# HGRN2 attention into a PReLU feed-forward layer: the usual steps without the one-column product that reads the moved keys

## The chip, the cores and the metric

One core of one Trainium2 chip runs the whole program. The metric is the device time of one execution in microseconds (us), the median of several runs. All matmuls are in float32, each of which the profile shows as two passes of a weight load and a matmul.

## The reference

The first part is a gated linear recurrence over 768 positions, for 4 batches and 8 heads of 48 values. The second part takes its output, 3072 rows of 384, through a feed-forward layer with 2048 hidden values and a learned slope for negative ones.

```python
def _attn_ref(q, k, v, f_logit) -> np.ndarray:
    B, H, S, D = q.shape                       # 4, 8, 768, 48
    f = 1.0 / (1.0 + np.exp(-f_logit))
    state = np.zeros((B, H, D, D), dtype=np.float32)
    y = np.zeros_like(q)
    for t in range(S):
        state = f[:, :, t, :, None] * state + np.einsum('bhd,bhe->bhde', k[:, :, t], v[:, :, t])
        y[:, :, t] = np.einsum('bhd,bhde->bhe', q[:, :, t], state)
    return y.astype(np.float32)

def _moe_ref(x, w_in, w_out, alpha) -> np.ndarray:
    h = x @ w_in
    g = np.maximum(h, 0.0) + alpha * np.minimum(h, 0.0)
    return (g @ w_out).astype(np.float32)
```

## The kernel before

The work is cut into 12 steps. A step is one chunk of 128 positions for a pair of batches; steps 2c and 2c + 1 belong to chunk c. Each step goes through three parts. *Preparation* loads the chunk, takes the sigmoid and forms running products of the gates (ScalarE and VectorE). *Attention* computes scores between queries and keys, the chunk's contribution to the state, and the output. *Network* takes the outputs of the step, laid out as `xT`, through both layers of the feed-forward part.

The recurrence needs the keys of a chunk with positions, not dimensions, along the partitions. From step 2 on this is done in two moves. VectorE transposes 32x32 blocks (word `kt`), and sixteen DMAs per step on SyncE's queue (word `km`, line 468) bring the blocks to their places in the tile `ksn`: four partition groups of the source (a) by four of the target (b). The sixteen DMAs are told of by eight semaphores, each used twice.

`ksn` is read on TensorE in two places. The *state products* (word `pd`, line 635, 64 matmul instructions per step) multiply keys and values into a PSUM tile `state`; each reads 48 of `ksn`'s columns on 64 of its partitions, and so blocks of four of the sixteen DMAs, and the first four products together read all sixteen. The *landed product* (word `kw`, line 641) is a product of one column of the identity with the four columns 0, 32, 64 and 96 of `ksn` on all partitions, one from each of the sixteen blocks. Its result, one row of four values, is never used: it goes into the PSUM bank that the next hidden-layer product (`n3` of the step before) then overwrites. `first` takes that bank from `ahead`, or a new one if there is none.

```python
        def keys_landed():
            to = ahead[n - 1, 3] = bank(f"phk_{i}")
            nc.tensor.matmul(to[0:1, 0:4], lhsT=ident[:, 0:1], rhs=x["ksn"][:, 0, 0:128:32], start=True, stop=True,
                             skip_group_check=True)
```

The order of the work is not left to a planner. It is written out by hand as a list of words, each with its step, and the program is emitted in that order, so that it is the order in which each engine's queue holds its instructions; an engine waits at an instruction until what that instruction needs is there. `FIRST` gives the words of the opening up to the end of step 3's attention and of step 2's network. `USUAL` gives the words of one step, and is used for n = 4 to 12 with words for a step that doesn't exist dropped; a word with `-` belongs to step n - 1, one with `+` to step n + 1. So in the usual order the network of step n - 1 runs between the attention of step n.

The words around the change, as TensorE sees them: `x0`, `x1` are scores of step n; `n0-` to `n7-` are the hidden-layer products of step n - 1 (line 763, 12 matmul instructions with 128x256 outputs each); `of` is a product within the chunk (line 597, 64 short matmuls, results copied by `oc0`, `oc1`); `pd` is the state products. Of the other engines, `g` is ScalarE's share and `G` VectorE's share of the activation that follows each `n`; `S0-` is four VectorE sums over gates; `m0` is VectorE's update of the running state, kept in `vs`, from the state products (lines 657 and 661). `A1`, `B` and so on are the output-layer products (line 859). `FIRST` has one `kw` of its own, for step 2. For step 3 it has `of:3 pd:3` and no `kw`. Values for steps 1 to 4 are loaded on GpSimd's queue, for the others on SyncE's.

Of the kernel before, what the change touches and what calls it, by code (L numbers as in the profile page):

```python
# [52 lines left out]
"""  # L53

USUAL = """
r0 R0 x0 X0 n0- g0- G0- n1- g1- G1- r1 R1 x1 X1 n2- g2- G2- kw n3- g3- G3- S0- of oc0 oc1 pd m0 n4- g4- G4- ld+ sg+ kr+ qc+ l1+ l2+ l3+ c0+ c1+ c2+
c3+ n5- g5- G5- n6- g6- G6- n7- g7- G7- S1- sc+ A1- B- ka- le+ k4+ e2+ p00A p01A p02A p03A p10A p11A p12A p13A y0 y1 C1- D- u2- ke+ kt+ e3+ e4+ sa+
e5+ m1 z0A z1A mv A2- C2- d0- oa- e6+ km+ e7+ sb+ fs+ E- u3- b- d1- s00+ s01+ s10+ s11+ e-
"""
# [929 lines left out]
```

## Time and profile before

| | |
|---|---|
| median of 3 runs | 617.76 us (615.91 to 619.95) |
| span of the profiled execution | 613.4 us |
| mean granted TensorE clock | 0.999 |
| hidden-layer products, line 763, tiles `ph` and `phk` | 948 and 108 matmul instructions |
| matmuls of line 641 | 18 (two passes each of nine products) |
| matmuls of line 635 on the tile `state` | 704 |
| like points of successive steps from step 5 on | some 47.3 us apart |

The span runs from the first to the last instruction of the program; the time of a run also holds what lies around it, here some 4.4 us by the median.

In the profile an engine's row names line, operation and tiles, out<-in. PE is TensorE's matmuls, PEld its weight loads, which run beside them, and PEldq its sequencer. DVE is VectorE, ACT ScalarE, POOL GpSimd, SP SyncE. The number of an instruction's durations is minimum/median/maximum in ns. Matmuls on small parts of the array run beside each other, so a group's busy time is less than count times duration. In brackets stands idle time before a group and what ended it; "issue" means that no wait the profile knows of ended it.

### The profile page before, as it was taken

To read this page: it belongs to the slowest core of one execution; us is meant where nothing else is said; L and a number is where in the kernel's file an instruction comes from. 1 tells how busy PE (TensorE), PEld (TensorE's weight loads), DVE (VectorE), ACT (ScalarE), POOL (GpSimd) and SP (SyncE) were. 2 spreads that over 40 slices of the span, in tenths; PEclk is the share of its full clock that TensorE was granted. 3 is DMA by queue.
4 is the path that set the end of the run, shared out by engine and by line. 5 is a ranking of instruction groups with operands and counts; after the bars stand their busy time and mean duration, and the time that the engine had idled before them with its cause. 6 is when DMAs were issued, how large, how long until landed. Compare 5 with 4: busy or idle time off the path is not lost.

```text
span 613.4 us, 18759 instructions
## 1 busy us (share of the span) xinstructions
PE 586.4 (96%) x8042; PEld 526.6 (86%) x8042; DVE 485.3 (79%) x993; ACT 242.5 (40%) x464; POOL 109.5 (18%) x154
## 2 busy tenths in 40 slices
PE   1689899999999999999999999999999999999997
PEld 1589766898999799899899899889899889889997
DVE  7988899985588789799899799789799889762251
ACT  5887732523412352361272271361362263223110
POOL 7437566298050000000000000000000000000000
PEclk9999999999999999999999999999999999999999
DMA  8996343141002502502502502502602601201000
GB/s 272 322 337 186 103 142 53 41 136 24 14 25 45 153 10 43 158 2 49 161 1 50 159 2 47 162 2 42 168 1 39 162 11 35 47 2 27 26 1 26
DMA packets 72002, 50.40 MB, mean 82 GB/s; under 512 B 47248, under 2 KB 62480, under 8 KB 71920
## 3 DMA queue, kind: packets, MB, share of 16 engines
q1 hardware_dynamic: 64464, 38.77, 23.6%
q0 software_dynamic: 2944, 8.59, 4.8%
q10 hardware_dynamic: 4512, 1.85, 1.2%
q8 instruction: 63, 1.03, 0.8%
q14 instruction: 19, 0.16, 0.1%
HBM read 36.21 MB, written 4.72 MB: 67 GB/s over the span
## 4 chain that ended last, share of the span: by engine, by line
PE 84%; DVE 6%; ACT 3%; issue 2%; POOL 2%; DMA 2%; POOLq 0%; ACTq 0%; DVEq 0%
PE ph L763 32%; PE pc L859 10%; PE pa L859 9%; PE pe L859 5%; PE pd L859 5%; PE pb L859 5%; PE py L694 4%; PE phk L763 4%; PE qu L514 3%; PE raw L493 3%; DMA q<-in_qT 2%; PE ph L781 2%; PE state L635 2%; PE off L597 1%; DVE w_out_sb L211 1%
## 5 line engine op out<-in xcount | busy, mean ns | idle before, releaser
L763 PE MATMUL ph<-xT,w_in_sb 128*128 128x256 f32 x948 | 213.0, 382 | 0.0
L763 PEld LDWEIGHTS ph<-xT,w_in_sb 128*128 128x128 f32 x948 | 177.7, 190 | 27.0 <-issue 1.7
L769 ACT ACTIVATE neg<-ph 128x512 f32<-128x512 f32 x79 | 46.3, 597 | 146.7 <-PE ph L763 110.7
L773 DVE SCALAR_TENSOR_TENSOR gate<-neg,om,ph 128x256 f32<-128x256 f32 x158 | 67.7, 476 | 40.5 <-ACT neg L769 39.5
L731 POOL DMA_DIRECT2D xT<-y x22 | 11.9, 546 | 392.0 <-ACT y L703 392.0
L859 PE MATMUL pa<-w_out_sb,gate 128*128 128x192 f32 x352 | 61.9, 328 | 0.1
L859 PE MATMUL pc<-t,S 128*128 128x192 f32 x352 | 61.7, 329 | 0.0
L859 PEld LDWEIGHTS pa<-w_out_sb,gate 128*128 128x128 f32 x352 | 57.9, 190 | 2.0 <-DVE gate L773 1.3
L859 PEld LDWEIGHTS pc<-t,S 128*128 128x128 f32 x352 | 57.3, 190 | 0.8 <-issue 0.2
L522 DVE COPY_PREDICATED ad<-mquad,qu 128x224 f32<-128x224 int32 (+6 forms) x140 | 42.0, 300 | 9.3 <-PE qu L514 3.2
L501 DVE COPY_PREDICATED ad<-mraw,raw 128x256 f32<-128x256 int32 (+1 forms) x96 | 42.4, 441 | 7.0 <-POOL A L680 2.8
L345 ACT COPY ut<-qd 128x256 f32<-128x256 f32 (+1 forms) x52 | 32.0, 634 | 23.2 <-DVE qd L211 12.1
L211 DVE TENSOR_TENSOR ut<-ut,fs 128x512 f32<-128x512 f32 (+6 forms) x64 | 38.5, 604 | 3.3 <-POOL ut L211 2.4
L429 ACT COPY A<-q 48x512 f32<-48x512 f32 x40 | 24.7, 616 | 35.2 <-DVE q L211 31.9
L882 ACT ACTIVATE o<-pa 128x192 f32<-128x192 f32 x11 | 3.6, 330 | 76.9 <-PE pa L859 76.9
L493 PE MATMUL raw<-qd,k 48*32 48x80 f32 x1536 | 22.4, 243 | 10.3 <-DVE qd L211 10.3
L493 PEld LDWEIGHTS raw<-qd,k 48*32 48x32 f32 x1536 | 18.1, 109 | 15.7 <-issue 15.5
L680 ACT COPY A<-ad 32x256 f32<-32x256 f32 x75 | 30.1, 401 | 1.1
L859 PE MATMUL pe<-w_out_sb,S 128*128 128x192 f32 x176 | 30.5, 327 | 0.0
L859 PE MATMUL pb<-t,gate 128*128 128x192 f32 x176 | 30.4, 326 | 0.0
L859 PE MATMUL pd<-w_out_sb,S 128*128 128x192 f32 x176 | 30.4, 326 | 0.0
L694 PEld LDWEIGHTS py<-A,vs 128*64 128x64 f32 x768 | 26.0, 145 | 4.0 <-issue 2.2
(138 smaller groups left out, 894.3 us busy)
## 6 DMA issues: line engine op xcount, KB each, us to landing
w_out_raw<-in_w_out SPq DMA_DIRECT2D x8, 767.8 KB, 5.5
w_in_raw<-in_w_in SPq DMA_DIRECT2D x8, 767.2 KB, 12.1
out<-o SPq DMA_DIRECT2D x24, 192.0 KB, 2.1
f<-in_fT SPq DMA_DIRECT2D x7, 512.0 KB, 4.3
q<-in_qT SPq DMA_DIRECT2D x7, 512.0 KB, 5.2
k<-in_kT SPq DMA_DIRECT2D x7, 512.0 KB, 6.9
vs<-in_v SPq DMA_DIRECT2D x14, 192.0 KB, 6.9
ksn<-kt SPq DMA_DIRECT2D x80, 32.0 KB, 2.0
```

Of the source, the lines that this page charges most:

```text
L211: (nc.gpsimd if beside[0] else nc.vector).tensor_tensor(*a)
L345: w[f"c{r}{mark}"] = lambda r=r: nc.scalar.copy(q4()[:, gs, :, r], qdv[r][:, gs, :, 0])
L429: copy(A[halves(cc)[1], u0:u1, par * HP:(par + 1) * HP, CH * cc:CH * (cc + 1)], x["q3"][rows(par)].rearrange("p (u h c) s t -> p u h c (s ...
L493: nc.tensor.matmul(to[DB * j:DB * (j + 1), par, hp * C:hp * C + QW], lhsT=x["k"][r_, g * DB:(g + 1) * DB], rhs=qd[r_, g], start=True, stop ...
L501: nc.vector.copy_predicated(adu[:, :, :, d:4], mraw[:, d, :, d:4].bitcast(I32).unsqueeze(1).broadcast_to((128, H, NB, n_)), rv[:, :, QO[d] ...
L522: nc.vector.copy_predicated(ad[:, u, :, :, 4 * m:DB], mquad[:, lo:lo + n_].bitcast(I32).unsqueeze(1).unsqueeze(1).broadcast_to((128, 2, HP ...
L680: copy(A[s_, u, :, s_], ad[s_, u].rearrange("p r h t -> p (r h) t"))
L694: nc.tensor.matmul(to[64 * par:64 * par + 64, u, o:o + CH], lhsT=vs[bp][:, cc, u, hd * D:hd * D + 64], rhs=A[:, u, par * HP + hp, CH * cc: ...
L763: nc.tensor.matmul(ph[f][:, j * T:(j + 1) * T], lhsT=w_in_sb[:, kt, m * 128:(m + 1) * 128], rhs=x["T"][:, kt], start=(kt == 0 and j == 0), ...
L769: nc.scalar.activation(neg[f], ph[f].rearrange("p (j t) -> p j t", j=2), AF.Relu, scale=-1.0)
L773: nc.vector.scalar_tensor_tensor(gate[:, m % NH, m // NH], neg[f][:, j], om[:, m:m + 1], ph[f].rearrange("p (j t) -> p j t", j=2)[:, j], A ...
L859: nc.tensor.matmul(p[name][:, 0:DH], lhsT=of(f), rhs=by(f), start=(f == 0 and not more), stop=(f == NH - 1), skip_group_check=True)
```

## The change

The word `kw` is taken out of `USUAL`, where it stood between `G2-` and `n3-`. Nothing else is touched: `kw:2` stays in `FIRST`, and so does the code of `keys_landed`.

```diff
 USUAL = """
-r0 R0 x0 X0 n0- g0- G0- n1- g1- G1- r1 R1 x1 X1 n2- g2- G2- kw n3- g3- G3- S0- of oc0 oc1 pd m0 n4- g4- G4- ld+ sg+ kr+ qc+ l1+ l2+ l3+ c0+ c1+ c2+
+r0 R0 x0 X0 n0- g0- G0- n1- g1- G1- r1 R1 x1 X1 n2- g2- G2- n3- g3- G3- S0- of oc0 oc1 pd m0 n4- g4- G4- ld+ sg+ kr+ qc+ l1+ l2+ l3+ c0+ c1+ c2+
 c3+ n5- g5- G5- n6- g6- G6- n7- g7- G7- S1- sc+ A1- B- ka- le+ k4+ e2+ p00A p01A p02A p03A p10A p11A p12A p13A y0 y1 C1- D- u2- ke+ kt+ e3+ e4+ sa+
 e5+ m1 z0A z1A mv A2- C2- d0- oa- e6+ km+ e7+ sb+ fs+ E- u3- b- d1- s00+ s01+ s10+ s11+ e-
 """
```

So the landed product is no longer run in steps 4 to 11, eight of its nine uses. In these steps `first` finds no bank in `ahead` for `n3` and takes one itself, and the first instructions on TensorE that read `ksn` are the state products.

## The prediction

> **What bounds the kernel now.** I read the page's busy times first, then the chain that ended last, then TensorE's timeline around one use of the product that goes away.
>
> ```profile
> PE 586.4 (96%) x8042; PEld 526.6 (86%) x8042; DVE 485.3 (79%) x993; ACT 242.5 (40%) x464; POOL 109.5 (18%) x154
> ...
> PE 84%; DVE 6%; ACT 3%; issue 2%; POOL 2%; DMA 2%; POOLq 0%; ACTq 0%; DVEq 0%
> ```
>
> TensorE is busy for 96% of the 613.4 us span and makes 84% of the chain; in the usual steps it hardly waits for anyone. So whatever lengthens or shortens its own queue there goes into the span one for one. The next two answers are its timeline in step 5 (start, us, group) and the instructions of the removed line 641 in the same stretch. PEldq is TensorE's sequencer; an EVENT_SEMAPHORE is an instruction of its own that only waits.
>
> ```profile
> 241.71 5.45 PE L763 MATMUL ph<-xT,w_in_sb 128*128 128x256 f32 x24
> 247.08 0.92 PE L493 MATMUL raw<-qd,k 48*32 48x80 f32 x64
> ...
> 248.77 2.86 PE L763 MATMUL ph<-xT,w_in_sb 128*128 128x256 f32 x12
> 251.56 0.20 PE L641 MATMUL phk<-ksn,ident 128*1 128x4 f32 x2
> 251.68 2.86 PE L763 MATMUL phk<-xT,w_in_sb 128*128 128x256 f32 x12
> 254.47 0.32 PE L597 MATMUL off<-q,kh 48*32 48x32 f32 x14
> ```
>
> ```profile
> L641 PEldq EVENT_SEMAPHORE  x4: 51/51/51, 248.6 to 248.9; - x4
> L641 PEld LDWEIGHTS phk<-ksn,ident x2: 80/82/83, 251.6 to 251.6; 128*1 128x1 f32 x2
> ```
>
> The reader is to see two things. First, the product's four wait instructions run at 248.6 to 248.9, three microseconds ahead of the product itself (251.56): the sequencer has already queued the twelve long matmuls of n2, so these waits cost TensorE nothing. Second, what the product does cost: n0 and n1, two such groups side by side without it, take 247.08 - 241.71 = 5.37 us from start to next start; n2, kw and n3 take 254.47 - 248.77 = 5.70 us.
>
> Are those waits ever long? The queue of the keys' transfers says no.
>
> ```profile
> L468 SPq DMA_DIRECT2D ksn<-kt x16: 604/610/1965, 233.2 to 244.4; - x16
> ...
> DMA to landing us min/median/max: 1.9/2.0/3.9
> ```
>
> Step 5's last transfer is issued at 244.4 and the slowest needs 3.9 us, so all have landed by 248.3 at the latest; the product comes 3.2 us later, the state products that truly read the keys (line 635) at 255.2. Every one of the 32 wait instructions of line 641 takes 51 ns, the least. So no wait for data is removed or added; what moves is the instructions that do the waiting.
>
> **Removed.** Eight of nine uses (steps 4 to 11; step 2 keeps its own in the written-out order): per step four waits, two weight loads, two matmuls of 168 ns, and the broken seam between n2 and n3. Gain per step: 5.70 - 5.37 = 0.33 us, all on TensorE's path. n3 takes its bank at n3 instead of just before it; no other allocation lies between, so no bank moves. No DMA is issued or moved, on SP's or POOL's queue or elsewhere.
>
> **Added.** Line 635 must now wait for the sixteen transfers itself. Its first four matmuls read four different sets of four transfers each, and the waits stand between them, in the middle of very short matmuls. The trace has this case: step 3 runs `of:3 pd:3` without kw. Below are line 635's waits and TensorE's timeline in step 3, then the same of step 5 (waits) and step 6 (timeline).
>
> ```profile
> L635 PEldq EVENT_SEMAPHORE  x9: 51/51/51, 150.4 to 151.5; - x9
> ```
>
> ```profile
> 149.94 0.76 PE L597 MATMUL off<-q,kh 48*32 48x32 f32 x64
> 150.77 1.74 PE L635 MATMUL state<-vs,ksn 64*48 64x48 f32 x64
> 152.43 1.35 PE L763 MATMUL ph<-xT,w_in_sb 128*128 128x256 f32 x5
> ```
>
> ```profile
> L635 PEldq EVENT_SEMAPHORE  x1: 51/51/51, 255.0 to 255.0; - x1
> ```
>
> ```profile
> 301.70 0.76 PE L597 MATMUL off<-q,kh 48*32 48x32 f32 x64
> 302.39 0.94 PE L635 MATMUL state<-vs,ksn 64*48 64x48 f32 x64
> 303.25 3.07 PE L763 MATMUL ph<-xT,w_in_sb 128*128 128x256 f32 x13
> ```
>
> Nine waits against one. From the start of `off` to the next long matmul it is 152.43 - 149.94 = 2.49 us in step 3 and 303.25 - 301.70 = 1.55 us in step 6: 0.94 us for eight more waits. None is longer than 51 ns in either step, so the 0.94 us is not data that came late. The cover is gone: the waits come out at 150.4, when the last of the 64 `off` matmuls starts at 150.5, and nothing is left in the queue to run.
>
> Bounds for this cost: at least 8 x 51 ns = 0.41 us (wait durations alone), at most step 3's 0.94. Step 3's values arrive by POOL's queue and its first and third matmuls wait for them too, which later steps may not need; a wait instruction takes up to two semaphores, so I still count three and two in front of these matmuls and nine in all. I take 0.94, the row of the same line, the same shapes and the same number of waits.
>
> [...]
>
> Queued behind these waits on TensorE are the 60 other state products and n4 to n7. VectorE first needs the states at line 661, at 307.1 in step 6 where they were done at 303.3: 3.8 us of slack against 0.94. ScalarE's copies of `off` come 0.33 us earlier.
>
> **Two steps differ.** In steps 4 and 9 the state products already stall inside:
>
> ```profile
> 208.54 0.30 PE L635 MATMUL state<-vs,ksn 64*48 64x48 f32 x6 [1.27 <-issue]
> ```
>
> The gap ended by "issue" in step 4 falls into a stretch in which the DMA engines are 89% busy (205.66 to 208.77) and the queue of instruction fetches moves two packets (205 to 210, 0.03 MB): I read it as TensorE's instructions coming late. From `off` to n4 step 4 takes 208.77 - 205.66 = 3.11 us, more than the 2.49 that the new waits alone would make. The waits then pass while the instructions are awaited: 0 added in step 4. Step 9 takes 445.46 - 443.74 = 1.72 us, 0.17 over step 6, and gets 0.77 instead of 0.94.
>
> **Sum.** Steps 5 to 8, 10 and 11: 6 x (0.94 - 0.33) = 3.66. Step 9: 0.77 - 0.33 = 0.44. Step 4: 0 - 0.33 = -0.33. Together +3.8 us: the profiled span goes from 613.4 to 617.2 us. What lies around the span is some 4.4 us (median 617.76 less 613.4) and is untouched, so the median goes to 617.8 + 3.8 = 621.6 us, +0.6%.
>
> **Rivals.**
> *The waits hide* (not slower). The sequencer would run ahead through `off` as it does through n2, and only the gain stays: 8 x 0.33 = 2.6, so 615.1 us. For it: 24 queued instructions covered the waits at n2, and `off` has 128. Against it: step 3, where the same `off` covered nothing. It holds if `off` to n4 stays at 1.55 us in step 6. [...] Chance 0.08.
> *The seam stays* (slower by over 1%). n3's first matmul would start as late without the product as with it, so that the 0.33 us is not given back: 8 x 0.33 = 2.6 us more than the sum, 3.8 + 2.6 = 6.4, so 624.2 us; with step 4 and 9 paying in full 8 x 0.94 = 7.5, 625.3 us. For it: the gap before `off` after n3 shows that group changes cost TensorE something. Against it: n0 and n1 have no seam. It passes 1% from 0.77 us net a step. Chance 0.13.
> *Instructions come late more often* (slower). Per step 8 instructions leave at kw and 8 come at line 635, so the block borders fall where they did for all but the stretch between; a border moved into a burst would cost some 1.3 us as in step 4, two of them 624.2 us. Chance 0.05.
> *It is absorbed* (no change). TensorE waits 1.3 us in all for the gates of A1 (line 859). Those gates hang on n4 to n7, behind the states, and move along; at the most 1.3 us of the 3.8 comes back: 620.3 us. Chance 0.06.
>
> **How the numbers follow.** The forecast has 0.68, its own range 619.8 to 623.4 (3.8 less half for a cost of the waits near the middle of their bounds, plus the steps 4 and 9 paying in full; the runs before spread by 2 us to either side). The range of 8 in 10 goes from 618.0 (wait costs at 0.41: 8 x 0.08 = 0.6 over before) to 625.2 (seam stays). Of 617.8, 1% is 6.2 us, about what a measurement of this kernel can tell from no change. Over 623.9 lie the seam, half of the late instructions and a little of the forecast's tail: 0.18. Below 611.6 lies next to nothing: the hidden waits reach 615.1 only, 0.02. The rest, 0.80, is within 1%.
>
> **What would show it.** Line 641 has 2 loads left instead of 18 and no wait at 51 ns; n2 and n3 appear as one group of 24 with 5.37 us to `off`. Line 635 has nine waits in each of steps 4 to 11, starting as `off` ends, and `off` to n4 takes 2.49 us in step 6. The distance between like points of successive steps grows from 47.3 to 47.9 us. Wrong it would be if that stretch stays at 1.55 us, if fewer waits appear, or if one of them is much longer than 51 ns, which would mean that transfers land late after all.

## The result and the profile after

The changed kernel takes 620.35 us (median of 22 runs, 618.02 to 625.25), the one before 618.48 us in the 22 runs beside it. The ratio is 1.0046, with a 95% interval of 1.0025 to 1.0067: 2.9 us slower, between 1.5 and 4.1. (The means, 620.81 and 618.01 us, lie 2.8 us apart, the medians 1.9.)

The profiled execution of the changed kernel spans 623.5 us, of the one before 613.4 us. Not all of that is the change: n2 of step 4, where the programs begin to differ, starts at 204.4 us against 200.0, after an opening that is the same code. The comparison of traces therefore goes from step 4 on. First the page's busy times and chain, then step 8 of the changed kernel in TensorE's timeline (start, us, group), and line 635's waits in that step.

```profile
PE 593.9 (95%) x8026; PEld 534.2 (86%) x8026; DVE 485.6 (78%) x993; ACT 242.1 (39%) x464; POOL 111.0 (18%) x154
...
PE 89%; ACT 3%; DMA 3%; DVE 2%; issue 2%; SPq 1%; ACTq 0%
```

```profile
398.87 5.45 PE L763 MATMUL ph<-xT,w_in_sb 128*128 128x256 f32 x24
404.25 0.76 PE L597 MATMUL off<-q,kh 48*32 48x32 f32 x64
405.07 1.58 PE L635 MATMUL state<-vs,ksn 64*48 64x48 f32 x64
406.58 1.78 PE L763 MATMUL ph<-xT,w_in_sb 128*128 128x256 f32 x7
```

```profile
L635 PEldq EVENT_SEMAPHORE  x9: 51/51/51, 404.8 to 405.7; - x9
```

TensorE is still the bound. n2 and n3 are one group of 24 that takes 5.38 us to the start of `off`, where n2, the removed product and n3 took 5.70. The nine waits are there, all of them of the shortest length, from 404.8 on, when the last short matmul of `off` starts. From `off` to n4 it is 406.58 - 404.25 = 2.33 us, against 1.55. So 0.78 us is paid and 0.32 us got back: 0.46 us more per step.

Step 4 behaves otherwise. Below are its timeline after the change and TensorE's busy time and granted clock (the figure of 0.88 or 1.00 ahead of the DMA share) over the 48 matmuls n4 to n7 that follow, first of the changed kernel, then of the one before.

```profile
209.80 0.76 PE L597 MATMUL off<-q,kh 48*32 48x32 f32 x64
210.63 1.55 PE L635 MATMUL state<-vs,ksn 64*48 64x48 f32 x58
213.82 0.40 PE L635 MATMUL state<-vs,ksn 64*48 64x48 f32 x6 [1.63 <-issue]
214.15 12.06 PE L763 MATMUL ph<-xT,w_in_sb 128*128 128x256 f32 x48
```

```profile
214.15:226.05 11.90, 11.90 (x51) 10.28 (x49) 6.72 (x11) 6.25 (x9) 0.00 (x0) 0.88 0.01 1
```

```profile
208.77:219.23 10.46, 10.46 (x53) 9.22 (x49) 7.95 (x14) 6.26 (x9) 0.00 (x0) 1.00 0.01 4
```

The stall in the middle of the state products is still there and longer (1.63 us, before 1.27), and the long matmuls behind it run for a while at half clock (a granted clock of 0.50 from 213.68 to 217.09 us, 3.41 us): the same 48 take 11.90 us instead of 10.46. A second profile of each kernel, further down, shows how much of this belongs to the change.

### The profile page after: what moved, and what is told of

It reads as the page before. It is cut to its first block, busy times and chain, and to the rows that moved or that the text cites. A ratio compares the mean times of both kernels' runs of the same rounds, so it can differ in the third digit from the quotient of the medians.

```text
span 623.5 us, 18759 instructions
## 1 busy us (share of the span) xinstructions
PE 593.9 (95%) x8026; PEld 534.2 (86%) x8026; DVE 485.6 (78%) x993; ACT 242.1 (39%) x464; POOL 111.0 (18%) x154
## 4 chain that ended last, share of the span: by engine, by line
PE 89%; ACT 3%; DMA 3%; DVE 2%; issue 2%; SPq 1%; ACTq 0%
PE ph L763 35%; PE pc L859 9%; PE pa L859 9%; PE pe L859 5%; PE pd L859 5%; PE pb L859 5%; PE py L694 4%; PE po L823 3%; PE qu L514 3%; PE raw L493 3%; PE state L635 3%; DMA w_in_raw<-in_w_in 3%; PE ph L781 2%; PE off L597 1%; PE xt L717 1%
## 5 line engine op out<-in xcount | busy, mean ns | idle before, releaser
L763 PE MATMUL ph<-xT,w_in_sb 128*128 128x256 f32 x1044 | 235.2, 383 | 0.0
L763 PEld LDWEIGHTS ph<-xT,w_in_sb 128*128 128x128 f32 x1044 | 197.0, 191 | 29.9 <-issue 1.5
L769 ACT ACTIVATE neg<-ph 128x512 f32<-128x512 f32 x87 | 51.1, 598 | 172.3 <-PE ph L763 124.1
L773 DVE SCALAR_TENSOR_TENSOR gate<-neg,om,ph 128x256 f32<-128x256 f32 x174 | 74.8, 477 | 55.4 <-ACT neg L769 52.9
L345 ACT COPY ut<-qd 128x256 f32<-128x256 f32 (+1 forms) x52 | 31.9, 633 | 23.8 <-DVE qd L211 12.2
```

What stands on the lines that cost most here:

```text
L345: w[f"c{r}{mark}"] = lambda r=r: nc.scalar.copy(q4()[:, gs, :, r], qdv[r][:, gs, :, 0])
L763: nc.tensor.matmul(ph[f][:, j * T:(j + 1) * T], lhsT=w_in_sb[:, kt, m * 128:(m + 1) * 128], rhs=x["T"][:, kt], start=(kt == 0 and j == 0), ...
L769: nc.scalar.activation(neg[f], ph[f].rearrange("p (j t) -> p j t", j=2), AF.Relu, scale=-1.0)
L773: nc.vector.scalar_tensor_tensor(gate[:, m % NH, m // NH], neg[f][:, j], om[:, m:m + 1], ph[f].rearrange("p (j t) -> p j t", j=2)[:, j], A ...
```

## The experiments

Theory: the change costs because a wait instruction holds TensorE's sequencer for about 0.1 us (0.78 us for eight in step 8), and at line 635 nothing long is queued that runs meanwhile, as there was at n2. Rivals: the state products are slow as first readers of the moved keys, wherever they stand; the seam of the removed product stays; instructions come late. The half product and the product of the identity start from the kernel before, *opening too* from the run with step 4 split, the others from the changed kernel; each diff is against the kernel it starts from, and `...` marks what is left out. The table gives the time from n2 to n4, read from the timelines' starts, for step 8 and for step 4.

| kernel | waits of line 635 per step | n2 to n4, step 8 | n2 to n4, step 4 | stall in step 4 | clock behind it |
|---|---|---|---|---|---|
| before, two profiles | 1 | 7.25, 7.25 | 8.80, 9.11 | 1.27, 1.58 | full, half |
| after, two profiles | 9 | 7.71, 7.71 | 9.72, 9.72 | 1.63, 1.60 | half, half |
| states first | 9 | 6.93 | 9.32 | 2.19 | half |
| half product | 5 | 7.59 | 9.48 | 1.57 | half |
| product of the identity | 9 | 8.06 | 9.63 | 1.35 | half |
| split bursts | 9 | 8.09 | 8.29 | 0.89 | full |
| step 4 split | 9 | 6.93 | 8.51 | 1.10 | full |
| opening too | 9 | 6.93 | 8.52 | 1.12 | full |

**The state products first.**

```diff
-... G3- S0- of oc0 oc1 pd m0 n4- ...
+... G3- S0- pd of oc0 oc1 m0 n4- ...
```

> Without kw, and the state products put ahead of `off` in the usual steps, right behind the twelve long matmuls of n3. Theory (the change costs because the new wait instructions stand among short matmuls, with nothing queued that runs meanwhile): the nine waits of line 635 come out while n3 is queued, and both products together take some 1.55 us a step again, not 2.35; only the removed product's 0.33 us a step is left: 8 x 0.33 = 2.6 us faster than the kernel before, some 616 us or ratio 0.996. Rival (the state products are slow wherever they stand, because they are now the first to read the moved keys or because their instructions come late): 2.35 us a step stays, and the ratio to before stays at 1.0046.

Measured: 615.81 us (12 runs), ratio to before 0.9984 (0.9954 to 1.0015). TensorE's timeline and line 635's waits in step 6:

```profile
299.25 5.45 PE L763 MATMUL ph<-xT,w_in_sb 128*128 128x256 f32 x24
304.63 0.94 PE L635 MATMUL state<-vs,ksn 64*48 64x48 f32 x64
305.50 0.76 PE L597 MATMUL off<-q,kh 48*32 48x32 f32 x64
306.18 1.99 PE L763 MATMUL ph<-xT,w_in_sb 128*128 128x256 f32 x8
```

```profile
L635 PEldq EVENT_SEMAPHORE  x9: 51/51/56, 300.7 to 302.1; - x9
```

The same nine waits now come out at 300.7 to 302.1, more than two microseconds before the states, while n2 and n3 run; and both bursts take 306.18 - 304.63 = 1.55 us, to the hundredth what they took before the change. Nothing but the order of the two bursts, and with it the place of the waits, was altered, so it is the place that cost 0.78 us. The rival of slow first readers falls. The time of the run fell less than expected, and its interval doesn't separate it from the kernel before: in this profile step 4 (9.32 us, half clock) gave back a good part of the gain. All 12 runs have a mean granted clock of 0.997 or less, where a profile without a stretch at half clock in it has 0.999 or more.

**Half of the waits at n2.** The product is back, in the usual steps on two columns of the keys instead of four, so that eight of the sixteen transfers are awaited there.

```diff
-            nc.tensor.matmul(to[0:1, 0:4], lhsT=ident[:, 0:1], rhs=x["ksn"][:, 0, 0:128:32], ...
+            nc.tensor.matmul(to[0:1, 0:(4 if n < FROM else 2)], lhsT=ident[:, 0:1], rhs=x["ksn"][:, 0, 0:(128 if n < FROM else 64):32], ...
```

> kw is back in its place but reads two columns of the moved keys, those of the first eight transfers, so that half of the waits stay at n2 and half go to line 635 (four more wait instructions there than before, by count, where the change has eight more). Theory (each uncovered wait instruction costs about 0.1 us): `off` to n4 takes 1.55 + 4 x 0.1 = 1.95 us a step, halfway between before and after; 8 x 0.4 = 3.2 us over the kernel before, ratio 1.005, with the seam's 0.33 us still paid. Rival (what costs is one late arrival or one first read, not the number of waits): 1.55 or 2.35 us, nothing in between.

Measured: 619.95 us (10 runs), ratio 1.0035 (1.0002 to 1.0067). Line 635's waits and the timeline in step 8:

```profile
L635 PEldq EVENT_SEMAPHORE  x5: 51/51/51, 403.7 to 404.1; - x5
```

```profile
403.16 0.76 PE L597 MATMUL off<-q,kh 48*32 48x32 f32 x64
403.85 1.27 PE L635 MATMUL state<-vs,ksn 64*48 64x48 f32 x64
405.05 2.21 PE L763 MATMUL ph<-xT,w_in_sb 128*128 128x256 f32 x9
```

`off` to n4 takes 1.89 us here, 1.92 to 2.05 in the other steps from 5 on but for step 7, where a gap of 0.39 us makes it 2.41. In step 8 four more waits cost 0.34 us, eight more 0.78: it goes by their number, near 0.09 to 0.10 us each. (The waits' own starts agree: the nine of the changed kernel lie between 404.8 and 405.7, some 0.11 us from one to the next.)

**A product that waits for nothing.** The product is back with the identity in the place of the keys.

```diff
-            nc.tensor.matmul(to[0:1, 0:4], lhsT=ident[:, 0:1], rhs=x["ksn"][:, 0, 0:128:32], ...
+            nc.tensor.matmul(to[0:1, 0:4], lhsT=ident[:, 0:1], rhs=x["ksn"][:, 0, 0:128:32] if n < FROM else ident[:, 0:4], ...
```

> kw is back in its place but multiplies four columns of the identity and waits for nothing, so only its matmuls and its seam return, and the waits stay at line 635 as in the changed kernel. Theory: n2 to `off` takes 5.70 us a step instead of 5.37, `off` to n4 some 2.35 us as after; 8 x 0.33 = 2.6 us over the changed kernel, ratio to before 1.0046 + 0.0043 = 1.009. Rival (the product costs through its waits, or its place is free): n2 to `off` stays at 5.37 us and the ratio at 1.0046.

Measured: 621.51 us (10 runs), ratio 1.0075 (1.0047 to 1.0103). In step 8:

```profile
395.97 2.86 PE L763 MATMUL ph<-xT,w_in_sb 128*128 128x256 f32 x12
398.76 0.19 PE L641 MATMUL phk<-ident 128*1 128x4 f32 x2
398.88 2.86 PE L763 MATMUL phk<-xT,w_in_sb 128*128 128x256 f32 x12
401.67 0.76 PE L597 MATMUL off<-q,kh 48*32 48x32 f32 x64
```

n2 to `off` is 401.67 - 395.97 = 5.70 us again, without any wait. So the product's 0.32 us is its matmuls and the broken seam, and the change does give it back; the rival of a seam that stays falls. The ratio came out lower than the expected 1.009, within its interval.

**The bursts apart.**

```diff
-... n2- g2- G2- n3- g3- G3- S0- of oc0 oc1 pd m0 ...
+... n2- g2- G2- of n3- g3- G3- S0- oc0 oc1 pd m0 ...
```

> Without kw, and `off` put between n2 and n3, so that the state products stand right behind n3's long matmuls and the two bursts of short matmuls lie apart. Theory: the waits are covered by n3 as in the run with the states first, and in step 4, where the instructions came late within the second burst (1.27 us before, 1.63 us after), the 2.7 us of n3 between the bursts give them time, so that this stall goes too; against that one more seam of some 0.2 us a step: 8 x (0.33 - 0.2) + 1.3 = 2.3 us faster than before, ratio 0.996. Rival (the late instructions of step 4 depend on the transfers of the next step's inputs alone and not on the bursts): the stall stays, and the ratio is 0.998.

Measured: 620.56 us (12 runs), ratio 1.0063 (1.0032 to 1.0093). This is a miss. What was expected of step 4 came in part (8.29 us, 0.89 us of stall, full clock) and n2 to n4 fell to 7.13 us in most steps. But steps 7 and 8 took 8.73 and 8.09 us, with new stalls ended by "issue", and the first product of the output layer waits more often for its gates. The waits by pairs (us in total, times, longest):

```profile
PEld pa L859 <- DVE gate L773: 5.4, 13, 0.5
```

Before it was 1.3 us in six, and with the states first, where the gain was larger, it is 1.3 us in six too. So it is the place of n3, rather than the gain, that turns into this wait. With `off` ahead of it n3 ends only the 0.86 us of the states before n4 starts, instead of 1.55, and VectorE, which works through the activations of n3 and their sums first, gets to n4 later: in step 9 its first instruction on n4 starts 5.66 us after n4, with the states first 4.96.

**Step 4 alone split, the states first elsewhere.**

```diff
-... G3- S0- of oc0 oc1 pd m0 n4- ...
+... G3- S0- pd of oc0 oc1 m0 n4- ...
...
-        for token in usual.split():
+        for token in (usual if n > FROM else usual.replace("G2- n3-", "G2- of n3-").replace("pd of oc0 oc1", "oc0 oc1 pd")).split():
```

> The states first as in the first run, but in step 4 alone `off` stands between n2 and n3 and the states behind n3. [...] Rival (stall and half clock of step 4 come by chance of the run and not from the order): 615.8 us and ratio 0.998 as with the states first.

The question comes from step 4 of the changed kernel: a stall of 1.63 us, 3.41 us at half clock, and 1.44 us more in the 48 matmuls behind it (11.90 against 10.46). With the bursts 2.7 us apart the author expected 8.3 us from n2 to n4, full clock behind it, and a run of 613.3 us, ratio 0.994.

Measured: 614.93 us (12 runs), ratio 0.9959 (0.9928 to 0.9991). Step 4 and the clock over its n4 to n7:

```profile
202.20 0.76 PE L597 MATMUL off<-q,kh 48*32 48x32 f32 x64
202.88 2.86 PE L763 MATMUL ph<-xT,w_in_sb 128*128 128x256 f32 x12
205.67 0.92 PE L635 MATMUL state<-vs,ksn 64*48 64x48 f32 x58
207.69 0.30 PE L635 MATMUL state<-vs,ksn 64*48 64x48 f32 x6 [1.10 <-issue]
207.92 10.63 PE L763 MATMUL ph<-xT,w_in_sb 128*128 128x256 f32 x48
```

```profile
207.92:218.38 10.46, 10.46 (x53) 9.23 (x49) 8.70 (x15) 6.24 (x9) 0.00 (x0) 1.00 0.02 6
```

In this profile the half clock is gone, and the run is faster than the kernel before and the changed one, though by less than expected (0.994). The stall is only shortened, to 1.10 us; that the distance of the bursts decides it is not shown. Nor is the half clock gone for good: the mean granted clock was 0.997 or less in 8 of these 12 runs.

**The opening too.** Step 3's states go ahead of its `off`, and step 2's product is left out.

```diff
-... km:2 pd:2 of:2 kw:2 n5:1 ...
+... km:2 pd:2 of:2 n5:1 ...
...
-... km:3 of:3 pd:3 p02V:3 ...
+... km:3 pd:3 of:3 p02V:3 ...
```

> As the run before this one, with the opening treated the same way: step 3's states ahead of its `off`, and step 2's landed product left out (there it comes after the state products and covers nothing). Theory: step 3 saves its nine uncovered waits, 0.8 us, and step 2 some 0.2 us: 1 us under the run before this one, ratio to before 0.993. Rival (the opening waits for other engines and hides 1 us): no difference between the two.

Measured: 613.65 us (12 runs), ratio 0.9930 (0.9898 to 0.9962). From n2 to the long matmuls behind the two bursts step 3 takes 6.84 us instead of 7.65 in the run with step 4 split, the expected 0.8; in step 2, from the states to the products of line 694, it is 6.93 us instead of 7.05, 0.12 and not 0.2. The times of the two kernels differ by 1.3 us with overlapping intervals, so the runs alone don't settle that part.

**The two kernels again**, for a second profile of each.

> The kernel before, unchanged, for a second profile. Theory (the stall of step 4 with its 3.4 us at half clock came with the change): n2 to n4 of step 4 at 8.8 us and full clock from step 4 on again. Rival (it comes by chance): in this profile the half clock may follow step 4, and n4 of step 4 to n4 of step 5 takes 48.7 us instead of 47.3.

> The changed kernel, unchanged, for a second profile. Theory: `off` to n4 at 2.35 us in the usual steps, and step 4 again with 9.7 us and the half clock behind it, as in all four runs so far that have the two bursts side by side and one of the new orders. Rival: step 4 without the half clock, n4 of step 4 to n4 of step 5 at 47.8 us instead of 49.1.

The kernel before took 616.97 us, the changed one 622.77, one run each. In the second profile of the kernel before, step 4 and the clock behind it:

```profile
208.80 0.30 PE L635 MATMUL state<-vs,ksn 64*48 64x48 f32 x6 [1.58 <-issue]
209.03 12.31 PE L763 MATMUL ph<-xT,w_in_sb 128*128 128x256 f32 x48
```

```profile
209.03:221.18 12.15, 12.15 (x53) 10.38 (x49) 7.67 (x13) 6.23 (x9) 0.00 (x0) 0.86 0.01 1
```

So the stall with half clock behind it can happen without the change; the rival holds for that. The changed kernel showed it in both profiles and repeated 9.72 us for step 4 and 7.71 us for step 8. But its other runs tell against a tie. A stretch of 3.41 us at half clock, worked out from its length, lowers the mean granted clock of a run by some 0.003. Of the 22 runs of the changed kernel 10 have a mean of 0.999 or more, and so no such stretch; of the 58 runs of the kernel before that were taken beside these experiments, 16. So the runs do not show the half clock as a cost of the change.

## Why the prediction was right, and where it was not

The forecast was +3.8 us, by waits that lose their cover. The measured +2.9 us lies in its range, on its side, and within 1%. By its steps:

- **Removed, 0.33 us a step.** Right: 0.32 in the changed kernel (5.38 against 5.70 us), and put back by the product of the identity alone.
- **No wait for data.** Right: all nine waits stay at 51 ns, as do those of the half product.
- **Added, 0.94 us a step.** The mechanism was right, the count of nine too (`x9` in step 8; in the trace of the kernel before 361 of all 707 wait instructions name two semaphores, 346 one, none more); the size was not: 0.78 us at step 8, 0.78 to 0.81 in steps 5, 7, 8 and 10. The row of step 3 held something else as well. Behind the first six matmul instructions of its state products stands a gap ended by "issue" (`151.49 0.13 issue` in the chain of that stretch). In the changed kernel's profile the same step 3 ran without it, in 2.36 us instead of 2.49, and in the second profile of the kernel before in 2.35. With 0.78 the net is 0.46 us a step instead of 0.61. A wait cost 0.78 / 8 = 0.098 us in step 8, though its own row shows 51 ns.
- **Step 4 pays nothing.** This step failed. The waits were to pass while instructions were awaited. Instead, n2 to n4 rose from 8.80 and 9.11 us to 9.72 us twice, although the product's 0.32 us was gone. The waits stand ahead of the first four state products and the gap behind the 58th of their 64 matmul instructions: the waits were paid first, and the gap behind them did not shrink (1.63 and 1.60 us against 1.27 and 1.58).
- **Step 9 pays less.** Right by luck: `off` to n4 went from 1.72 to 2.38 us, 0.66 more, but the 0.17 us on which this rests was one execution's. In the second profile of the kernel before, step 9 takes 1.55 us like the others, and the second of the changed kernel is 0.82 above it. Steps 6 and 11 took 0.94 more in the first profile, from a gap of 0.13 us in each.
- **The sum.** From n2 to n4 the steps 5 to 11 together take 54.4 us in both profiles of the changed kernel and 50.9 and 50.8 us in those of the kernel before: 3.5 us. Step 4 adds 0.6 to 0.9. That is some 4.2 us. That the predicted 3.8 lies so near is luck, two errors that nearly cancel: the steps 5 to 11 cost 3.5 us and not the 4.1 forecast for them, step 4 adds 0.6 to 0.9 us instead of giving back 0.33. The 4.2 us lie at the upper edge of what the runs measured, 1.5 to 4.1. What gives back a part in the runs is not shown: the opening differs between executions of one kernel by more than that, and the kernel before lost time to the half clock at least as often. Between runs at a mean clock of 0.999 or more the distance is 2.6 to 4.5 us (618.6 against 614.1 and 616.0 us, medians; the two rounds of the kernel before are not the ones beside this result). A slip in the range: its lower end of 618.0 is 618.4 by its own sum, 617.8 + 0.6.
- **The rivals.** *The waits hide* was the wrong reading of this change, but true of another place: behind n3 they did hide. To wait later than at n2 paid only there, 6.93 us from n2 to n4 against 7.25; later still, among the short matmuls, it made 7.71. *The seam stays* is refuted. *Instructions come late more often* was seen in small, as gaps of 0.13 us in two steps; the gap of step 4 is in every profile, before and after. *It is absorbed* hardly showed: the waits for the gates at line 859 are 0.9 and 1.3 us in the two profiles after, 1.3 in both before, so at most 0.4 us came back.

## What to carry to other kernels

A wait that never waits still cost the sequencer's time here, about 0.1 us each (0.78 us for eight), and that time was free only with long matmuls queued ahead: both bursts took 1.55 us with the states first, 2.33 us in the changed kernel. Count the wait instructions that a change moves, and look at what stands in the queue ahead of them; to move the first reader of many transfers right behind long matmuls did all that the extra product had done, without the product (6.93 us from n2 to n4 against 7.25). A single row taken as the price of a step can hold another, smaller stall: look inside it first.

## What the runs showed of the hardware that was not expected

TensorE's clock fell to half for 3.41 us at the end of the stall of step 4, or up to 0.8 us behind it, in six of the ten profiles, and the 48 long matmuls behind it then took 11.8 to 12.2 us instead of 10.46. In these profiles it followed stalls of 1.35 us and longer (1.35, 1.57, 1.58, 1.60, 1.63, 2.19) and none of the shorter ones (0.89, 1.10, 1.12, 1.27). A stall of 1.40 us in step 7 of the run with the bursts apart went by at full clock, so the length alone does not decide it; that the stall is the cause is not shown either, only that the half clock came with it or just behind it. With the 1.44 us more in the matmuls behind it, the stall of 1.63 us in the changed kernel goes with an estimated 3.1 us in all.

The stall of step 4 has its place in TensorE's instructions and not in the work. In all ten profiles it comes after the same 6081 instructions of TensorE in the trace (weight loads, matmuls and waits together): 58 matmul instructions into the second burst, 56 in the two kernels whose product adds four instructions before it, 60 in the one whose opening has four fewer, and inside `off` where `off` is the second burst. The new stalls of the split bursts come after 9921 and 11201 instructions, 15 and 20 times 256 further, and so does the 0.39 us of the half product, after 9921. A packet of 16384 bytes on the queue of instruction fetches lands shortly before TensorE goes on: 206.85 against 208.54 us in the kernel before, 208.70 against 209.99 with the product of the identity. This fits the reading that instructions come late, block by block; the place is shown, the cause is inferred.

Why they come late at this border is open. The next inputs are being loaded at the time, but over the gap itself the DMA engines were busy 78% in the first profile of the kernel before and not at all with the product of the identity (208.6 to 210.0). And the border after 9921 instructions, in step 7, made 1.40 us, 0.39 us or no such gap, by the kernel. Moving the loads away, or a border out of the burst, was not tried.
